# One loop over all decode units, one joining of the heads, and weights on 112 partitions

## The chip, the cores and the metric

The kernel runs on one core of a Trainium2 chip. The metric is the device time of one execution in microseconds. A time is the median of several runs; a profile is one further execution, recorded instruction by instruction and transfer by transfer.

## What is computed

One decode step for two sequences: an attention block over a cached key/value store and a two-layer ReLU network share the input `x` (2 x 448) and are mixed by a gate.

```python
g = sigmoid((x * gate_w).sum(-1, keepdims=True))
q = (x @ wq).reshape(2, 1, 16, 256).transpose(0, 2, 1, 3)
p = softmax(q @ k_cache^T * 256 ** -0.5)      # k_cache: 2 x 16 x 4096 x 256
a = (p @ v_cache) -> 2 x 1 x 4096 @ wo        # v_cache: 2 x 16 x 4096 x 256
b = relu(x @ w1) @ w2                         # w1: 448 x 1792, w2: 1792 x 448
out = g * a + (1 - g) * b
```

Everything is float32. The caches are 268 MB of the 290 MB that have to be read.

## The kernel before

A *unit* is one head of one sequence: 32 units. The host lays each out as 128 rows of 64 KB, the keys in the first half of a row, the values in the second (`kv[u]`). SBUF holds three such *slots* (`slot[0..2]`); unit u lies in slot u % 3.

**SyncE (SP)** issues all large loads. First wq into slot 2, then units 0 and 1 (L122 to L124), then in a loop of ten rounds with three units each the units 2 to 31 (`more`, L126). Before each refill it takes `free[s]`, which VectorE gives after the last use of the slot. Then `late` (L141): w1, the eight pieces `w1x`, and w2 into slot 2 once unit 29 is done there; wo in five pieces (`CUTS`) into slot 0 once unit 30 is done there. All of these go through one queue, in this order, over the core's 16 transfer engines. ScalarE issues only the small `xg` (x and gate_w).

448 input rows are laid out as three blocks of 128 and one of 64 (`KF` = 3 full blocks, `HP` = 64): the last block stands twice in `xg`, and the halves of wq and w1 that belong to it are spread over the upper and the lower 64 partitions, so that both weights fill 128 partitions (56 KB and 24.5 KB on each). `w1x` holds the last 448 columns of w1: those of the upper 64 partitions are laid on the lower 64 (`MOVE`), in eight transfers of eight partitions each.

**A unit** passes four engines. TensorE (`scores`, L243) waits for the slot (`land[s]`), for the unit's query and for `room` in the PSUM tile `ps`, and makes 4096 scores as 4 groups of 1024, each group repeated on 32 partitions. VectorE (`values`, L268) takes the maximum (L270); ScalarE (`softmax`, L261) takes the exponential (L263) and copies the next query into `query[s]` (`pick`, L257); VectorE multiplies the values with the probabilities and sums them, in eight instructions (L274), into `ov`. The first of them gives `room`, the last gives `free[s]`. TensorE, ScalarE and VectorE run this in ten rounds of three units; units 30 and 31 follow unrolled.

**Before the loop**: the gate by small matmuls (L196 to L208), the queries by wq in two halves (`NB` = 2, L217), each with transposes through `ident`. `xr` and `xu` are copies of x spread over columns, made by VectorE (L176, L178).

**The heads are joined twice** (`combine`, L294), for units 0 to 15 between the loop and the last two units, for units 16 to 31 at the end: two transposes of maxima and sums, the common maximum, exponentials, weights `wb` (with the gate in them), a matmul that spreads them, the weighting `os`, and matmuls with `sel` that sum the groups into `ot`.

**The end**: w1 (L336 to L345), ReLU, transposes, then 14 blocks of w2 and 24 blocks of wo are accumulated in the PSUM tile `acc`, the last eight blocks of wo directly in `z` (`project`, L372), while the second `combine` runs step by step between the wo blocks. `acc` is folded into `z`, copied and stored.

Every wait is written out: `pr.op` counts an engine's instructions in a semaphore of its own, and `take` waits on a semaphore and lowers it again.

Of the kernel before, what the change touches and what calls it, by code (L numbers as in the profile page):

```python
# [8 lines left out]
P, HP = 128, 64  # L9
G = 4  # L10
R = P // G
SLOTS = 3
NB = 2
ENGINES = ("tensor", "vector", "scalar", "gpsimd", "sync")


class Program:

    def __init__(self, nc):
        self.nc = nc
        self.code = {e: [] for e in ENGINES}
        self.count = dict.fromkeys(ENGINES, 0)

    def op(self, engine, fn, *after):
        self.count[engine] += 1  # L30
        self.code[engine].append(("op", fn, after))
        return engine, self.count[engine]

    def raw(self, engine, fn, *after):
        self.code[engine].append(("raw", fn, after))

    def loop(self, engine, n, fn):
        self.code[engine].append(("loop", n, fn))

    def emit(self, block, sems):  # L40
        def run(name):
            def body(e):
                seen = {}
                for kind, a, b in self.code[name]:
                    if kind == "loop":
                        with e.Fori(0, a) as i:
                            b(e, i)
                        continue
                    for who, n in b:
                        if seen.get(who, 0) < n:  # L50
                            e.wait_ge(sems[who], n)
                            seen[who] = n
                    if kind == "op":
                        a(e).then_inc(sems[name], 1)
                    else:
                        a(e)
            return body

        for name in ENGINES:
            getattr(block, name)(run(name))  # L60
# [7 lines left out]
def gated_mix_decode(nc, xg, kv, wq, w1, w1x, w2, wo, out):  # L68
    U, _, LEN = kv.shape
    KC, B = xg.shape[1], xg.shape[2] - 1  # L70
    KF = KC - 1
    D = KF * P + HP
# [5 lines left out]
    SG = S // G  # L78
    NF = w2.shape[1] // D
    DG = D // G  # L80
    FG = NF * P // G
    RB = R // B
    HB = H // NB
    UB = U // NB
    HH = HB // G
    CW = 512
    SCALE = float(DH) ** -0.5
    LOOPS = (U - 2) // SLOTS
    assert U == LOOPS * SLOTS + 2 and SLOTS == 3

# [3 lines left out]
    def bank(name, n=CW):  # L94
        return nc.alloc_psum_tensor(name, [P, n], F32).ap()

    NO = NB * HH * J
    CUTS = (0, NO - 18, NO - 8, NO - 4, NO - 1, NO)
    TAIL = 8
    names = [*ENGINES, "xg", "w1x", "w2", *(f"wo{k}" for k in CUTS[1:]), "query", "score", "top", "prob", "room",  # L100
             *(f"land{s}" for s in range(SLOTS)), *(f"free{s}" for s in range(SLOTS)), "out"]
    sem = {n: nc.alloc_semaphore(n) for n in names}
    land = [sem[f"land{s}"] for s in range(SLOTS)]
    free = [sem[f"free{s}"] for s in range(SLOTS)]
    pr = Program(nc)
    pe, dve, act, pool, sp = ENGINES


    sbuf("gap", P, -(-(-nc.sbuf_base // 32) * 32) % 1024 // 4)
    slot = [sbuf(f"slot{s}", P, LEN) for s in range(SLOTS)]  # L110
    ps = bank("ps", SG)
    pw = [bank(f"pw{k}") for k in range(4)]
    acc = bank("acc")[:, :D]


    def load(s, src, signal, lo=0, hi=None):
        hi = src.shape[1] if hi is None else hi
        return lambda e: e.dma_start(slot[s][:, lo:hi], src[:, lo:hi]).then_inc(signal, 16)  # L118

    xg_sb = sbuf("xg_sb", P, KC, B + 1)  # L120
    pr.raw(act, lambda e: e.dma_start(xg_sb, xg).then_inc(sem["xg"], 16))
    pr.raw(sp, load(2, wq, land[2]))  # L122
    for u in range(2):
        pr.raw(sp, load(u, kv[u], land[u]))  # L124

    def more(e, i):  # L126
        for k in range(SLOTS):
            s = (2 + k) % SLOTS
            take(e, free[s])
            src = kv[bass.ds(i * SLOTS + (2 + k), 1)].rearrange("o p n -> (o p) n")  # L130
            e.dma_start(slot[s], src).then_inc(land[s], 16)

    pr.loop(sp, LOOPS, more)

    W1, WX = w1.shape[1], w1x.shape[2]
    w1_sb, w1x_sb = slot[2][:, :W1 + WX], slot[2][:, W1:W1 + WX]
    w2_sb = slot[2][:, W1 + WX:W1 + WX + NF * D]

    def late(e):  # L141
        take(e, free[2])
        load(2, w1, land[2])(e)
        for k in range(8):
            o = k // 4 * 4 * 8 + k % 4
            e.dma_start(w1x_sb[o:o + 4 * 7 + 1:4], w1x[k]).then_inc(sem["w1x"], 16)
        e.dma_start(w2_sb, w2).then_inc(sem["w2"], 16)
        take(e, free[0])
        for lo, hi in zip(CUTS, CUTS[1:]):
            load(0, wo, sem[f"wo{hi}"], lo * D, hi * D)(e)  # L150
        take(e, free[1])

    pr.raw(sp, late)

    ident = sbuf("ident", P, P)

    have_ident = pr.op(pool, lambda e: e.memset(ident, 0.0))
    have_ident = pr.op(pool, lambda e: e.affine_select(
        out=ident, in_=ident, compare_op=ALU.not_equal, fill=1.0, base=0, pattern=[[-1, P]], channel_multiplier=1),
        have_ident)  # L160


    sel = sbuf("sel", P, R)
    t = pr.op(dve, lambda e: e.tensor_reduce(sel, ident.rearrange("p (g r) -> p r g", g=G), axis=AX.X, op=ALU.add),
              have_ident)
    fsum = sbuf("fsum", P, B)
    t = pr.op(dve, lambda e: e.tensor_reduce(fsum, sel.rearrange("p (b r) -> p b r", b=B), axis=AX.X, op=ALU.add), t)
    fold = sbuf("fold", P, B, RB)
    have_fold = pr.op(dve, lambda e: e.tensor_scalar(fold, fsum[:, :, None].to_broadcast([P, B, RB]), 1.0 / RB, None,
                                                     op0=ALU.mult), t)  # L170


    xr = sbuf("xr", P, KC, G, B, RB)
    pr.raw(dve, lambda e: e.wait_ge(sem["xg"], 16))
    for g in range(G):
        pr.op(dve, lambda e, g=g: e.tensor_copy(xr[:, :, g], xg_sb[:, :, :B, None].to_broadcast([P, KC, B, RB])))  # L176
    xu = sbuf("xu", P, KC, UB // B, B)
    have_x = pr.op(dve, lambda e: e.tensor_copy(xu, xg_sb[:, :, None, :B].to_broadcast([P, KC, UB // B, B])))  # L178

    def rows_of(c, i=0):  # L180
        return slice(0, P) if c < KF else slice(i * HP, (i + 1) * HP)

    def flat(a):
        return a.rearrange("p b r -> p (b r)")

    def mm(out, lhs, rhs, start, stop, *after):
        return pr.op(pe, lambda e: e.matmul(out, lhs, rhs, start=start, stop=stop), *after)  # L187

    def transpose(out, src, *after):
        return pr.op(pe, lambda e: e.transpose(out, src, ident), *after)  # L190

    def activate(out, src, fn, *after, **kw):
        return pr.op(act, lambda e: e.activation(out, src, fn, **kw), *after)  # L193


    pr.raw(pe, lambda e: e.wait_ge(sem["xg"], 16))  # L196
    for c in range(KC):
        r = rows_of(c)
        t = mm(pw[0][:, :1], xr[r, c].rearrange("p g b r -> p (g b r)"), xg_sb[r, c, B:], c == 0, c == KC - 1, have_x)
    gp = sbuf("gp", P, 1)  # L200
    gate_read = t = activate(gp, pw[0][:, :1], AF.Sigmoid, t)
    omg = sbuf("omg", P, 1)
    have_omg = pr.op(dve, lambda e: e.tensor_scalar(omg, gp, -1.0, 1.0, op0=ALU.mult, op1=ALU.add), t)
    for c in range(KC):
        r = rows_of(c)
        t = mm(pw[1][:UB, :1], xu[r, c].rearrange("p u b -> p (u b)"), xg_sb[r, c, B:], c == 0, c == KC - 1)
    gu = sbuf("gu", UB, 1)
    have_gu = activate(gu, pw[1][:UB, :1], AF.Sigmoid, t)  # L208


    qt = sbuf("qt", P, T, U)
    W = 2 * KF * DH
    WQ = wq.shape[1] // NB
    wide = sbuf("wide", P, CW)
    pr.raw(pe, lambda e: take(e, land[2], 16))
    busy = [(), ()]
    for i in range(NB):  # L217
        w = slot[2][:, i * WQ:(i + 1) * WQ]
        for c in range(KC):
            for g in range(G):  # L220
                r = rows_of(c, g // 2)
                at = g * W + c * CW if c < KF else G * W + g % 2 * CW
                lhs, rhs = flat(xr[r, c, g]), w[r, at:at + CW]
                last = mm(pw[2 + i][g * R:(g + 1) * R, :], lhs, rhs, c == 0, c == KC - 1)
        t = activate(wide, pw[2 + i], AF.Copy, last, *busy[1], scale=SCALE)
        pt = pw[i]
        for k in range(2 * T):
            t2 = transpose(pt[:, k * P:(k + 1) * P], wide[:, k * P:(k + 1) * P], t, gate_read, have_gu)
        busy[1] = (t2,)
        for s in range(2):  # L230
            dst = qt.rearrange("p t (i g s b) -> p i s t g b", i=NB, g=G, s=2)[:, i, s]
            src = pt[:, ::RB].rearrange("p (s t g b) -> p s t g b", s=2, t=T, g=G)[:, s]
            have_q = activate(dst, src, AF.Copy, t2)

    nm = sbuf("nm", P, U)
    ls = sbuf("ls", P, U)
    ov = sbuf("ov", P, U, J)
    prob = sbuf("prob", P, SG)  # L240
# [20 lines left out]
    def softmax(e, u, s, more=True):  # L261
# [3 lines left out]
        if more:  # L265
            pick(e, u + 1, (s + 1) % SLOTS)
# [200 lines left out]
```

## Time and profile before

| | |
|---|---|
| median of 3 runs | 675.29 us (675.29 to 675.54) |
| span of the profiled execution | 674.6 us |
| moved in it | 289.66 MB, 429 GB/s over the span |
| busy: VectorE, TensorE, ScalarE | 341.5, 224.6, 59.7 us |
| TensorE clock granted | 0.648 of full speed |

The span runs from the first to the last instruction of the profiled execution; the runs' times have about 0.7 us more around it. In the views below, PE is TensorE (PEld its weight loads), DVE is VectorE, ACT ScalarE, POOL GpSimd and SP SyncE; `L274` is line 274 of the kernel; `out<-in` are the program's names. A group's row gives the number of its instructions, busy microseconds and the mean of one in nanoseconds, then the idle time ahead of them and what ended it. A row of the timeline or of the chain begins with its start and its length in microseconds. A row of a stretch gives start and end, its length, busy time and instructions of PE, PEld, DVE, ACT and POOL, the granted clock, the share of time that the 16 transfer engines were busy, and GB/s. A row of a load gives its size and the microseconds from issue to landing.

### The profile page before, as it was taken

How to read it: one execution, taken by the hardware profiler on the slowest of the kernel's cores; microseconds unless marked ns; L12 is line 12 of the kernel's file. 1: busy time of each engine (PE TensorE's matmuls, PEld its weight loads, DVE VectorE, ACT ScalarE, POOL GpSimd, SP SyncE). 2: the span in 40 equal slices, each digit the busy share in tenths (PEclk: the TensorE clock that was granted, in tenths of full speed). 3: DMA queues.
4: the chain of work that ended last, by engine and by line, in shares of the span. 5: the costliest groups of instructions: out<-in, count | busy, mean ns of one | idle time of the engine just before them, and what ended most of it. 6: DMA issues, size and time to landing. Idle time of an engine off the chain costs nothing. (4 is left out here: it accounts for less than half of the span.)

```text
span 674.6 us, 4166 instructions
## 1 busy us (share of the span) xinstructions
PE 224.6 (33%) x1323; PEld 67.0 (10%) x1323; DVE 341.5 (51%) x571; ACT 59.7 (9%) x121; POOL 0.7 (0%) x6
## 2 busy tenths in 40 slices
PE   0643221333332123333322333333222333321277
PEld 0210000001001000100100010010001001000022
DVE  0006566544556664455566545455665544657652
ACT  0020001001000100100010010000001001000010
POOL 0000000000000000000000000000000000000000
PEclk9975567667655666765566676665567666556688
DMA  9999999999999999999999999999999999999997
GB/s 381 428 435 436 436 435 435 435 435 435 435 431 435 435 435 435 435 431 435 435 435 435 435 435 435 435 435 435 435 435 435 435 431 427 435 427 435 400 444 316
DMA packets 6180, 289.66 MB, mean 429 GB/s; under 512 B 992, under 2 KB 1120, under 8 KB 1440
## 3 DMA queue, kind: packets, MB, share of 16 engines
q1 hardware_dynamic: 6032, 289.60, 99.3%
q8 instruction: 3, 0.05, 0.0%
q10 hardware_dynamic: 144, 0.01, 0.0%
q14 instruction: 1, 0.01, 0.0%
HBM read 289.54 MB, written 0.06 MB: 429 GB/s over the span
## 5 line engine op out<-in xcount | busy, mean ns | idle before, releaser
L274 DVE SCALAR_TENSOR_TENSOR slot<-slot,prob 128x1024 f32<-128x1024 f32 x256 | 295.9, 1222 | 65.1 <-DVEq L65 65.1
L251 PE MATMUL ps<-slot,query 128*32 128x512 f32 x1024 | 190.8, 909 | 404.4 <-PEq L65 404.3
L270 DVE TENSOR_REDUCE nm<-ps 128x1024 f32 (+1 forms) x32 | 39.2, 1225 | 230.8 <-DVEq L65 230.8
L251 PEld LDWEIGHTS ps<-slot,query 128*32 128x32 f32 x1024 | 54.7, 158 | 539.1 <-issue 539.0
L263 ACT ACTIVATE prob<-ps,nm 128x1024 f32<-128x1024 f32 x32 | 35.6, 1113 | 385.0 <-ACTq L65 384.9
L263 ACT ACT_TABLE_LOAD x10 | 12.8, 1283 | 163.4 <-ACTq L65 163.4
L274 DVE DVE_READ_ACCUMULATOR slot<-slot,prob (+1 forms) x256 | 21.3, 83 | 0.0
L187 PE MATMUL pw<-slot,xr 128*32 128x512 f32 (+3 forms) x96 | 12.9, 671 | 1.3 <-DMA slot<-in_w1x 1.3
L176 DVE COPY xr<-xg_sb 128x128 f32<-128x128 f32 x4 | 0.6, 224 | 18.0 <-DMA xg_sb<-in_xg 18.0
L187 PE MATMUL pw<-xg_sb,xr 128*128 128x1 f32 (+1 forms) x8 | 1.9, 352 | 21.2 <-DVE xu L178 21.2
L187 PE MATMUL acc<-slot,ot 128*32 128x448 f32 x48 | 7.2, 661 | 2.3 <-DMA slot<-in_wo 2.2
L258 ACT ACTIVATE query<-qt 128x2 f32 (+1 forms) x32 | 6.2, 193 | 0.0
L263 ACT ACTIVATION_READ_ACCUMULATOR prob<-ps,nm (+1 forms) x32 | 6.2, 193 | 0.0
L187 PE MATMUL acc<-slot,hr 128*32 128x448 f32 x28 | 4.9, 810 | 2.0 <-DMA slot<-in_w 2.0
L190 PE MATMUL pw<-ident,nm 128*16 128x128 f32 x2 | 0.7, 328 | 12.6 <-DVEq L324 12.6
L187 PEld LDWEIGHTS pw<-xg_sb,xr 128*128 128x128 f32 (+1 forms) x8 | 1.8, 321 | 21.2 <-DMA xg_sb<-in_xg 21.2
L187 PEld LDWEIGHTS pw<-slot,xr 128*32 128x32 f32 (+1 forms) x96 | 2.8, 122 | 9.9 <-issue 7.7
L190 PE MATMUL pw<-ident,wide 128*128 128x128 f32 x11 | 1.9, 288 | 2.4 <-ACT wide L193 2.4
L310 DVE TENSOR_TENSOR os<-ov,pw 128x128 f32<-128x128 f32 x2 | 0.6, 287 | 4.0 <-PE pw L187 4.0
L318 DVE COPY ot<-pw 128x256 f32<-128x256 f32 x4 | 1.5, 420 | 2.0 <-PE pw L187 2.0
L391 DVE COPY wide<-acc 128x448 f32<-128x448 f32 x1 | 0.6, 624 | 3.1 <-PE pw L187 3.1
L187 PE MATMUL pw<-slot,ot 128*32 128x112 f32 x64 | 2.0, 261 | 0.2 <-DMA slot<-in_wo 0.2
(42 smaller groups left out, 20.9 us busy)
## 6 DMA issues: line engine op xcount, KB each, us to landing
slot<-in_wq SPq DMA_DIRECT2D x1, 7168.0 KB, 19.4
slot<-in_w SPq DMA_DIRECT2D x1, 3136.0 KB, 29.9
slot<-in_wo SPq DMA_DIRECT2D x1, 3136.0 KB, 21.2
slot<-in_w SPq DMA_DIRECT2D x1, 2912.0 KB, 28.2
slot<-in_wo SPq DMA_DIRECT2D x1, 2240.0 KB, 26.1
slot<-in_wo SPq DMA_DIRECT2D x1, 896.0 KB, 27.8
slot<-in_wo SPq DMA_DIRECT2D x1, 672.0 KB, 28.9
slot<-in_kv SPq DMA_DIRECT2D x32, 38.4
```

The costliest lines, as they stand in the source:

```text
L176: pr.op(dve, lambda e, g=g: e.tensor_copy(xr[:, :, g], xg_sb[:, :, :B, None].to_broadcast([P, KC, B, RB])))
L187: return pr.op(pe, lambda e: e.matmul(out, lhs, rhs, start=start, stop=stop), *after)
L190: return pr.op(pe, lambda e: e.transpose(out, src, ident), *after)
L251: m = e.matmul(ps[g * R:(g + 1) * R, c * CW:(c + 1) * CW], query[s][:, t:t + 1].to_broadcast([P, R]), slot[s][:, lo:lo + CW], start=(t == ...
L258: e.activation(query[s], qt[:, :, bass.ds(u, 1)].rearrange("p t o -> p (t o)"), AF.Copy).then_inc(sem["query"], 1)
L263: e.activation(prob, ps, AF.Exp, bias=nm[:, bass.ds(u, 1)], accum_out=ls[:, bass.ds(u, 1)]).then_inc(sem["prob"], 1)
L270: e.tensor_reduce(nm[:, bass.ds(u, 1)], ps, axis=AX.X, op=ALU.max, negate=True).then_inc(sem["top"], 1)
L274: m = e.scalar_tensor_tensor(v, v, 1.0, prob, op0=ALU.mult, op1=ALU.mult, accum_out=ov[:, bass.ds(u, 1), j])
L310: t = pr.op(dve, lambda e: e.tensor_tensor(os, ov[:, us], wp[:, :UB, None].to_broadcast([P, UB, J]), op=ALU.mult), t)
L318: t = pr.op(dve, lambda e, hh=hh: e.tensor_copy(ot[:, i, hh], po[:, hh * B * J:(hh + 1) * B * J].rearrange("p (b j o) -> p j b o", j=J, o= ...
L391: t = pr.op(dve, lambda e: e.tensor_copy(a_sb, acc), t)
```

## The change

The program is written anew engine by engine, without the counting class. What it does otherwise:

- `x`, wq and w1 are laid out as four blocks of 112 rows (448 = 4 x 112) on 112 partitions: wq is 64 KB and w1 28 KB on each. `w1x` is gone. kv, w2 and wo stay on 128 partitions.
- The gate's sums are made by GpSimd and one matmul with ones; GpSimd also makes `xr`, then `ident`, and `xo` (x times 1 - g), so that the ReLU network's part of the gate is in its input. The attention's part of the gate is applied when `lhs` is written.
- All 32 units run in one loop: eleven rounds on TensorE, the third unit of a round under a test; on VectorE and ScalarE one unit a round. VectorE computes the slot's address from the unit's number.
- There is one `query` tile and no `room`.
- The last unit's keys and values are two transfers with a semaphore each (`land[1]`, `late`); VectorE waits for the values before it multiplies.
- All 32 units are joined once: TensorE transposes maxima and sums after the last exponential, VectorE does the softmax part between the last unit's products (after the fourth and the seventh, under tests of the unit's number), and the rest follows after the loop. All 24 + 8 wo blocks come after it.
- wo comes in pieces of 14, 6, 4, 4, 3 and 1 blocks (before: 14, 10, 4, 3 and 1).

```diff
-P, HP = 128, 64
+P, KP = 128, 112
...
-        for k in range(8):
-            o = k // 4 * 4 * 8 + k % 4
-            e.dma_start(w1x_sb[o:o + 4 * 7 + 1:4], w1x[k]).then_inc(sem["w1x"], 16)
...
+    def sync(e):
+        bring(e, slab(2, 0, KC * NQ * G * CW, KP), wq, sem["wq"])
+        for u in range(2):
+            bring(e, slot[u], kv[u], land[u])
+        with e.Fori(0, U // SLOTS) as i:
+            for k in range(SLOTS):
+                take(e, sem["free"])
+                s = (k + 2) % SLOTS
+                src = kv[bass.ds(i * SLOTS + (k + 2), 1)].rearrange("o p n -> (o p) n")
+                if k < SLOTS - 1:
+                    bring(e, slot[s], src, land[s])
+                    continue
+                with e.If(i == U // SLOTS - 1):
+                    bring(e, slot[s][:, :T * S], src[:, :T * S], land[s])
+                    bring(e, slot[s][:, T * S:], src[:, T * S:], sem["late"])
+                with e.Else():
+                    bring(e, slot[s], src, land[s])
+        take(e, sem["free"])
+        bring(e, slab(2, 0, KC * F, KP), w1, sem["w1"])
+        bring(e, slab(2, W2, LEN), w2, sem["w2"])
+        take(e, sem["free"])
+        for lo, hi in zip(WO, WO[1:]):
+            bring(e, slab(0, (lo - NF) * D, (hi - NF) * D), wo[:, (lo - NF) * D:(hi - NF) * D], sem[f"wo{hi}"])
...
+    def gpsimd(e):
+        e.memset(ones, 1.0)
+        e.memset(qt[:, :, U:], 0.0)
+        e.wait_ge(sem["xg"], 16)
...
+        e.tensor_copy(xc4, xg_sb[:KP, :, :B, None].to_broadcast([KP, KC, B, RB]))
+        settle(e, sem["pool"], e.memset(ident, 0.0))
...
+        with e.Fori(0, -(-U // SLOTS)) as i:
+            for s in range(SLOTS - 1):
+                scores(s)
+            with e.If(i < U // SLOTS):
+                scores(SLOTS - 1)
+        take(e, sem["query"])
+        e.transpose(tp[:U, :P], nm, ident)
+        e.transpose(tp[:U, P:2 * P], ls, ident).then_inc(sem["tr"], 1)
+        take(e, sem["xo"])
+        take(e, sem["w1"], 16)
+        project(xo, 0, F)
+        take(e, sem["wb"])
...
+        with e.Fori(0, U) as u:
+            take(e, sem["score"], G)
+            e.tensor_reduce(nm[:, bass.ds(u, 1)], ps, axis=AX.X, op=ALU.max, negate=True).then_inc(sem["top"], 1)
+            take(e, sem["prob"])
+            with e.If(u == U - 1):
+                e.wait_ge(sem["late"], 16)
+            for j in range(J):
+                v = ring[:, bass.ds((u % SLOTS) * LEN + (T * S + j * SG), SG)]
+                m = e.scalar_tensor_tensor(v, v, 1.0, prob, op0=ALU.mult, op1=ALU.mult,
+                                           accum_out=ov[:, bass.ds(u, 1), j])
+                if j == 3:
+                    with e.If(u == U - 1):
+                        take(e, sem["tr"])
+                        e.tensor_reduce(nb, mt, axis=AX.X, op=ALU.min).then_inc(sem["nb"], 1)
+                if j == 6:
+                    with e.If(u == U - 1):
+                        take(e, sem["e4"])
...
+            m.then_inc(sem["free"], 1)
+        settle(e, sem["vec"], e.drain())
+        take(e, sem["wp"])
+        e.tensor_tensor(os, ov, wp[:, :, None].to_broadcast([P, U, J]), op=ALU.mult).then_inc(sem["os"], 1)
...
-    w1x = np.concatenate([w1[:HP, -MOVE:], w1[HP:, -MOVE:]], 1)
...
+        return a.reshape(KC, KP, -1).transpose(1, 0, 2)
...
+    wq = rows(wq.reshape(D, -1)).reshape(KP, -1)
...
+    w1 = rows(B_w1).reshape(KP, -1)
```

`bring` is a transfer with its semaphore, `settle` an instruction that its own engine waits for, `slab(s, lo, hi, rows)` a part of slot s.

## Prediction before the changed kernel was run

> **What bounds the kernel now.** I read the page first: its DMA lines, the chain that ended last and the costliest groups.
>
> ```profile
> span 674.6 us, 4166 instructions
> ...
> DMA  9999999999999999999999999999999999999997
> GB/s 381 428 435 436 436 435 435 435 435 435 435 431 435 435 435 435 435 431 435 435 435 435 435 435 435 435 435 435 435 435 435 435 431 427 435 427 435 400 444 316
> ...
> q8 instruction: 3, 0.05, 0.0%
> ...
> DMA slot<-in_wo 4%; SPq L118 0%; PE pw L187 0%; DVE res L397 0%
> ...
> L274 DVE SCALAR_TENSOR_TENSOR slot<-slot,prob 128x1024 f32<-128x1024 f32 x256 | 295.9, 1222 | 65.1 <-DVEq L65 65.1
> ...
> slot<-in_wq SPq DMA_DIRECT2D x1, 7168.0 KB, 19.4
> ...
> slot<-in_w SPq DMA_DIRECT2D x1, 2912.0 KB, 28.2
> ...
> slot<-in_kv SPq DMA_DIRECT2D x32, 38.4
> slot<-in_w1x SPq DMA_DIRECT2D x8, 28.0 KB
> ```
>
> The transfer engines are busy in every slice and the chain ends in the loading of wo; no compute engine is above 51%. Stretches of the span, with the DMA share and GB/s last, show where anything could be won:
>
> ```profile
> 0.00:20.20 20.20, 0.00 (x0) 0.00 (x0) 0.74 (x3) 1.28 (x1) 0.70 (x6) 1.00 1.00 416
> 20.20:39.50 19.30, 13.04 (x88) 5.02 (x88) 0.89 (x6) 2.25 (x9) 0.00 (x0) 0.96 1.00 435
> 39.50:620.50 581.00, 179.10 (x962) 51.71 (x962) 314.61 (x513) 52.00 (x101) 0.00 (x0) 0.62 1.00 433
> 620.50:639.80 19.30, 7.40 (x42) 2.27 (x42) 10.62 (x21) 1.30 (x3) 0.00 (x0) 0.59 0.96 415
> 639.80:655.80 16.00, 10.73 (x79) 3.10 (x83) 8.73 (x16) 2.65 (x6) 0.00 (x0) 0.82 1.02 437
> 655.80:671.60 15.80, 13.38 (x124) 4.20 (x116) 5.64 (x15) 0.26 (x1) 0.00 (x0) 0.79 0.92 387
> 671.60:674.60 3.00, 0.97 (x32) 0.71 (x32) 0.27 (x1) 0.00 (x0) 0.00 (x0) 1.00 0.08 21
> ```
>
> From 20 to 656 us the stream runs at its plateau of 435 GB/s. One unit (8192 KB, 8.39 MB) takes 8.39/0.435 = 19.3 us; wq (7168 KB, 7.34 MB) 16.9 us; w1 with w1x (2912 + 8 x 28 = 3136 KB, 3.21 MB) 7.4 us. The change moves the same bytes, so nothing in compute counts unless it makes this stream pause or slow down.
>
> **Units in one loop, VectorE unit by unit: nothing.** One unit in the steady part, in the timeline:
>
> ```profile
> 331.16 58.34 SPq L131 DMA_DIRECT2D slot<-in_kv  x4
> ...
> 331.29 5.41 PE L251 MATMUL ps<-slot,query 128*32 128x512 f32 x32 [12.86 <-PEq L65]
> ...
> 336.99 1.23 DVE L270 TENSOR_REDUCE nm<-ps 128x1024 f32 x1 [6.08 <-DVEq L65]
> 338.40 1.28 ACT L263 ACT_TABLE_LOAD   x1 [16.90 <-ACTq L65]
> ...
> 350.31 0.08 DVE L274 DVE_READ_ACCUMULATOR slot<-slot,prob  x1
> ...
> 350.67 5.88 PE L251 MATMUL ps<-slot,query 128*32 128x512 f32 x32 [13.97 <-PEq L65]
> ```
>
> VectorE works from 336.99 to 350.39, 13.4 of 19.3 us: 5.9 us a unit are free. The unit's slot is free 19.1 us after its keys came; the refill lies 38.4 us in the queue, of which 19.3 are its own transfer, so another 19.1 us could pass before the queue runs dry. Added per unit: three tests and a computed slot address on VectorE, a loop end on VectorE and ScalarE, and a table load in each unit instead of in one of three (1.28 us by its row). The tests have no row; bounds are 0 and, at one VectorE instruction (1.22 us) each, 3.7 us. With the table load that is 5.0, under 5.9: I take 0. Without that cover each microsecond over it would cost 32 us. The semaphore "room" goes, since the next scores wait for a query that is copied only after the exponential has read them; PE starts no later by it.
>
> **The start: nothing.** The same timeline, from xg's arrival:
>
> ```profile
> 20.34 0.63 DVE L176 COPY xr<-xg_sb 128x128 f32<-128x128 f32 x4 [18.04 <-DMA xg_sb<-in_xg]
> ...
> 23.46 5.78 PE L187 MATMUL pw<-slot,xr 128*32 128x512 f32 x32
> ...
> 36.19 24.03 SPq L131 DMA_DIRECT2D slot<-in_kv  x2
> 39.88 5.97 PE L251 MATMUL ps<-slot,query 128*32 128x512 f32 x32 [4.03 <-PEq L65]
> ```
>
> The four copies into xr, the copy into xu and two sets of gate matmuls go; seven GpSimd instructions stand between xg's arrival and the query products instead, and the transposes wait for ident, now made behind xg on the same engine. GpSimd's own rows lie at 0.1 to 0.3 us (0.70 for six in the first stretch); taking 0.1 and 1.22 as bounds, seven cost 0.7 to 8.5 us against the 3.1 us that now pass from 20.34 to 23.46: at most 5.4 later. Waiting behind it are SP's refill of slot 2, issued at 36.19, and the first scores. The queue still holds two units (20.2 + 38.6 = 58.8), 22 us of cover. If it were gone, the excess would be lost once.
>
> **The end: nothing from joining once, or from keys and values apart.** The timeline from unit 29's last product on:
>
> ```profile
> 619.67 5.48 SPq L146 DMA_DIRECT2D slot<-in_w1x  x8
> ...
> 641.15 0.08 DVE L274 DVE_READ_ACCUMULATOR slot<-slot,prob 128x1 f32 x1
> 641.33 2.23 SPq L118 DMA_DIRECT2D slot<-in_wo  x5
> ...
> 647.04 1.23 DVE L270 TENSOR_REDUCE nm<-ps 128x1 f32<-128x1024 f32 x1 [5.80 <-DVEq L65]
> ...
> 658.90 0.09 DVE L274 DVE_READ_ACCUMULATOR slot<-slot,prob 128x1 f32 x1
> ...
> 660.38 0.15 DVE L301 TENSOR_REDUCE nb<-pw 16x1 f32<-16x4 f32 x1 [1.39 <-PE pw L190]
> ...
> 662.53 1.72 PE L187 MATMUL acc<-slot,ot 128*32 128x448 f32 x8 [2.19 <-DMA slot<-in_wo]
> ...
> 666.10 4.19 PE L187 MATMUL acc<-slot,ot 128*32 128x448 f32 x32
> ...
> 666.54 0.76 DVE L318 COPY ot<-pw 128x256 f32<-128x256 f32 x2 [1.43 <-PE pw L187]
> ```
>
> The chain that ended last, in order of time, closes so:
>
> ```profile
> 642.65 28.93 DMA slot<-in_wo
> 671.59 0.04 issue
> 671.63 1.10 PE pw L187 x32
> ```
>
> With keys 9.6 us ahead, unit 31's scores run under unit 30's products (end 641.23), and its own 11.9 us on VectorE (647.04 to 658.99) start there: 653.2. Joining now takes from 660.38 to 667.3, 6.9 us with waits for PE; double width on all of it would be 13.8, and 667.0. Without the wo products that PE now slips in between, and with the softmax part moved into the value loop, I take 5 to 6, near 659. The first piece of wo lands at 662.5: 3.5 us of cover. Queued behind the wait for ot are 24 wo blocks (48 passes; 32 took 4.19 us by the same timeline, about 6.3 in all) and the closing products; late by the upper bound they would still be fed by pieces that land until 671.6, so the tail would grow by 2 us at most. VectorE's new waits for "late", "tr" and "e4" hold the rest of unit 31's products and only PE's joining behind them. On SP eight issues (5.48 us) go and two come (0.33 to 0.43 each), all while it waits for slots. Moving 224 KB of w1 to the lower 64 partitions is undone: 14 KB for each of eight engines, 0.5 us at 27.2 GB/s (435/16), either way; I take 0.
>
> **112 partitions: 12.1 us.** The bytes stay, but wq becomes 64 KB on each of 112 partitions instead of 56 KB on 128, w1 28 KB instead of 24.5. The trace has no 112-partition load; the w1x pieces are its only narrow ones, and at 640 to 656 us, where they pass, the rate is 437. Lower bound: equal bytes, equal time, 0 (not below: the stream already stands on its plateau). Next: time follows the bytes of one partition. A unit's 64 KB take 19.3 us, so wq takes 19.3, +2.4, and w1 8.4, +1.05: **+3.5**. [...]
>
> [...]
>
> **Sum:** span 674.6 + 0 + 0 + 0 + 12.1 = 686.7; the median of the runs shown (675.29) lies 0.7 above the span: **687.4 us**.
>
> **The rivals.** *Bytes of a partition alone* (+3.5): 678.8. For it: the unit's 19.3 us at 64 KB. Against it: it needs engines that never hold each other up. *112 partitions cost nothing* (0): 675.3. For it: w1x passes without a dent. Against it: those pieces are 224 KB beside the 128-partition w2. *Faster:* the stretches 620.5 to 639.8 and 655.8 to 671.6 move 415 and 387 GB/s; if w1x's eight issues and the uneven ends that they leave make this loss, dropping them gives back up to 19.3 x 20/435 + 15.8 x 48/435 = 2.6 us, 672.7; it decides only where 112 partitions cost under 1.3. Against it: the small last pieces of wo stay. *Code fetched again in each turn of the loops:* three 16 KB code packets now (0.05 MB); one a unit on one engine is 0.6 us at 27.2 GB/s, 32 x 0.6 = 19.3, 694.6. Or VectorE's 5.9 us are passed by one, 707. Against both: three-unit bodies fetch almost nothing today. [...]
>
> **Chances.** Held-up engines (own range 682 to 692) 0.52, a partition's bytes 0.26, no cost 0.12, faster 0.04, fetches or VectorE 0.06. A measurement of this kernel can tell 0.2% (1.35 us): slower 0.52 + 0.26 + 0.06 + 0.02 of the no-cost case = 0.86; same 0.10; faster 0.04. The range takes in the second case and most of the first: 676 to 692.
>
> **What would show it.** Right: the rate falls well below 416 GB/s in the first 20 to 30 us and again where w1 loads, the first unit's scores start some 8 us after 39.88, refills still reach landing after about 38 us, and the chain still ends in wo. Half right: wq 2.4 us later and no more. Wrong: a plateau unchanged at both places. Units more than 19.3 us apart with VectorE never waiting, or many more code packets, would be the last rival.

## Result: 22 us slower, nearly all of it where 112 partitions are loaded

| | median | runs | ratio to before, 95% interval |
|---|---|---|---|
| before | 675.54 us | 5 (675.29 to 675.86) | |
| changed | 697.41 us | 5 (695.85 to 699.88) | 1.0327 (1.0307 to 1.0346) |

The profiled execution of the changed kernel took 695.85 us, with a span of 694.5 us (674.6 before). A time lies 1.3 us above its span here and in every run that lists both; the 0.7 given with the kernel before compares a median with the span of another execution. The page of the changed kernel:

```profile
span 694.5 us, 4431 instructions
...
DMA  9999999999999999999999999999999999999997
GB/s 242 242 449 427 449 427 423 442 434 449 427 423 434 442 449 423 427 430 442 434 442 427 423 445 430 449 427 423 442 434 449 427 423 434 442 449 406 341 357 303
...
q8 instruction: 3, 0.05, 0.0%
```

The transfer engines count as busy in every slice, as before, but in the first two slices they move 242 GB/s, where the kernel before moved 381 and 428, and in slices 38 and 39 they move 341 and 357, where it moved 400 and 444. So a busy share near one says that engines have work, not that it flows: below, the share is 1.03 at 259 GB/s. Between, the plateau is the old one. The number of code packets is unchanged.

The two dents are the two loads on 112 partitions. The loads of the changed kernel, with size and us from issue to landing (the row `in_w` is w1 and w2 together):

```profile
ring<-in_w SPq DMA_DIRECT2D x2, 3136.0 KB, 36.5
...
ring<-in_kv SPq DMA_DIRECT2D x31, 37.7
...
ring<-in_wq SPq DMA_DIRECT2D x1, 33.4
```

Its stretches, with start and end, length, busy time of PE, PEld, DVE, ACT and POOL, granted clock, share and GB/s:

```profile
1.80:33.40 31.60, 0.00 (x0) 0.00 (x0) 0.00 (x0) 0.00 (x0) 0.00 (x0) 1.00 1.03 259
...
34.20:53.50 19.30, 10.53 (x78) 3.65 (x80) 0.74 (x3) 3.24 (x8) 1.67 (x7) 0.93 1.00 435
53.50:635.00 581.50, 173.09 (x968) 43.65 (x972) 314.39 (x510) 77.43 (x120) 0.00 (x0) 0.64 1.00 434
...
650.60:666.00 15.40, 0.58 (x2) 0.14 (x2) 12.02 (x21) 2.83 (x5) 0.00 (x0) 0.54 1.00 250
```

wq lands 33.4 us after its issue, against 19.4 before: 14.0 us. While w1's rows move (650.6 to 666.0), the rate is 250 GB/s. In the 600 us between, unit follows unit at the old rate.

The timeline of the changed kernel, from xg's arrival, through its first unit, and at the end:

```profile
34.38 0.20 POOL L145 TENSOR_TENSOR pg<-xg_sb 112x8 f32<-112x8 f32 x1 [33.39 <-DMA xg_sb<-in_xg]
...
37.72 5.11 PE L169 MATMUL ph<-ring,xr 112*32 112x512 f32 x32 [1.69 <-PEq L19]
...
53.46 5.77 PE L184 MATMUL ps<-ring,query 128*32 128x512 f32 x32 [4.01 <-PEq L19]
59.58 1.23 DVE L277 TENSOR_REDUCE nm<-ps 128x1024 f32 x1 [22.16 <-DVEq L19]
61.00 1.28 ACT L256 ACT_TABLE_LOAD   x1 [11.12 <-ACTq L19]
...
73.30 0.08 DVE L283 DVE_READ_ACCUMULATOR ring<-ring,prob  x1
73.33 6.08 PE L184 MATMUL ps<-ring,query 128*32 128x512 f32 x32 [14.10 <-PEq L19]
...
676.36 1.23 DVE L302 TENSOR_TENSOR lhs<-po,gate 128x1024 f32<-128x1024 f32 x1 [0.76 <-DVEq L19]
681.75 4.72 PE L221 MATMUL acc<-ring,lhs 128*32 128x448 f32 x40 [1.04 <-DMA ring<-in_wo]
...
690.93 0.98 PE L232 MATMUL z<-ring,lhs 128*32 128x112 f32 x32
692.48 0.27 DVE L308 COPY res<-z 128x112 f32<-128x112 f32 x1 [3.81 <-DVEq L19]
```

The first unit's scores start at 53.46 instead of 39.88, 13.6 us late, and the queue never regains it. The last products start at 690.93 instead of 671.63, 19.3 us late: 5.7 us more were lost on the way, most of them at w1, whose rows take 1.9 us each by the median where they take 1.06 in the padded kernel below. The remaining 0.6 of the span's 19.9 us lie behind them.

### The profile page after: what moved, and what is told of

It reads as the page before. It is cut to its first block, busy times and chain, and to the rows that moved or that the text cites. A ratio compares the mean times of both kernels' runs of the same rounds, so it can differ in the third digit from the quotient of the medians.

```text
span 694.5 us, 4431 instructions
## 1 busy us (share of the span) xinstructions
PE 214.4 (31%) x1294; PEld 56.9 (8%) x1294; DVE 339.1 (49%) x556; ACT 87.3 (13%) x140; POOL 2.1 (0%) x13
## 5 line engine op out<-in xcount | busy, mean ns | idle before, releaser
L283 DVE SCALAR_TENSOR_TENSOR ring<-ring,prob 128x1024 f32 x256 | 296.0, 1221 | 105.4 <-DVEq L19 105.4
L184 PE MATMUL ps<-ring,query 128*32 128x512 f32 x1024 | 183.3, 881 | 416.9 <-PEq L19 416.9
L277 DVE TENSOR_REDUCE nm<-ps 128x1024 f32 x32 | 39.2, 1225 | 189.2 <-DVEq L19 189.2
L184 PEld LDWEIGHTS ps<-ring,query 128*32 128x32 f32 x1024 | 46.2, 155 | 553.3 <-issue 553.3
L283 DVE DVE_READ_ACCUMULATOR ring<-ring,prob x256 | 21.1, 82 | 0.0
L221 PE MATMUL acc<-ring,lhs 128*32 128x448 f32 x76 | 10.3, 628 | 1.5 <-DMA ring<-in_wo 1.5
L169 PE MATMUL ph<-ring,xr 112*32 112x512 f32 x64 | 8.8, 696 | 1.7 <-PEq L19 1.7
L169 PE MATMUL ph<-ring,xo 112*32 112x512 f32 x32 | 6.2, 952 | 8.8 <-PEq L19 8.8
L256 ACT ACTIVATION_READ_ACCUMULATOR prob<-ps,nm x32 | 6.2, 193 | 0.0
L221 PEld LDWEIGHTS acc<-ring,lhs 128*32 128x32 f32 x76 | 2.8, 123 | 8.3 <-issue 4.6
## 6 DMA issues: line engine op xcount, KB each, us to landing
ring<-in_kv SPq DMA_DIRECT2D x31, 37.7
```

The lines of the kernel that those rows point to most:

```text
L169: m = e.matmul(ph[g * R:(g + 1) * R], x[:KP, c], slab(2, at, at + CW, KP), start=c == 0, stop=c == KC - 1)
L184: m = e.matmul(ps[g * R:(g + 1) * R, c * CW:(c + 1) * CW], query[:, t:t + 1].to_broadcast([P, R]), slot[s][:, at:at + CW], start=t == 0, s ...
L221: m = e.matmul(acc[g * R:(g + 1) * R], lhs[:, k], w, start=k < G, stop=k >= N - DIRECT - G)
L256: e.activation(prob, ps, AF.Exp, bias=nm[:, bass.ds(u, 1)], accum_out=ls[:, bass.ds(u, 1)]).then_inc(sem["prob"], 1)
L277: e.tensor_reduce(nm[:, bass.ds(u, 1)], ps, axis=AX.X, op=ALU.max, negate=True).then_inc(sem["top"], 1)
L283: m = e.scalar_tensor_tensor(v, v, 1.0, prob, op0=ALU.mult, op1=ALU.mult, accum_out=ov[:, bass.ds(u, 1), j])
```

## Experiments

**One part undone: 128 partitions in the new kernel.** Everything of the rewrite stays; x, wq and w1 are laid out in three full blocks and one half block.

```diff
-P, KP = 128, 112
+P, HP = 128, 64
...
-                    at = base + c * step + g * CW
-                    m = e.matmul(ph[g * R:(g + 1) * R], x[:KP, c], slab(2, at, at + CW, KP), start=c == 0,
+                    at = base + c * step + g * CW if c < KF else last + g % 2 * CW
+                    r = slice(0, P) if c < KF else slice(g // 2 * HP, (g // 2 + 1) * HP)
+                    m = e.matmul(ph[g * R:(g + 1) * R], x[r, c], ring[r, 2 * LEN + at:2 * LEN + at + CW], start=c == 0,
```

> The rewritten kernel with everything kept but x, wq and w1 laid on 128 partitions again (three full blocks and one half block, its halves on the upper and lower 64; w1 padded by 64 columns on each partition instead of the eight w1x pieces). Theory A, the 112 partitions alone cost the 22 us: about 675.5 us, within 1.5 of the kernel before, and the first unit's scores start again near 40 us. Rival R, the one loop, the single joining and the gate on GpSimd cost a part: it stays above 677, by as much as they cost.

Measured: 676.63 us (10 runs, 676.24 to 676.94), ratio 1.0009 (1.0000 to 1.0019). Its first unit's scores start where they did in the kernel before:

```profile
39.91 5.82 PE L187 MATMUL ps<-ring,query 128*32 128x512 f32 x32 [3.83 <-PEq L20]
```

Of the 21.9 us, 20.8 go with the 112 partitions. Theory A holds within its 1.5 us; rival R's 677 is not reached, but about a microsecond stays. (w1's padding is 128 columns on each partition, not 64: 3200 KB instead of 3136, worth 0.15 us at 435 GB/s.)

**112 rows loaded as 128.** The four blocks of 112 stay, products and all; the loads bring 16 rows of zeros along.

```diff
-        bring(e, slab(2, 0, KC * NQ * G * CW, KP), wq, sem["wq"])
+        bring(e, slab(2, 0, KC * NQ * G * CW), wq, sem["wq"])
...
-        bring(e, slab(2, 0, KC * F, KP), w1, sem["w1"])
+        bring(e, slab(2, 0, KC * F), w1, sem["w1"])
...
+    wq, w1 = (np.concatenate([a, np.zeros((P - KP, a.shape[1]), a.dtype)]) for a in (wq, w1))
```

> The rewritten kernel with its four blocks of 112 rows, but 16 rows of zeros are loaded too, so that wq and w1 are 128-partition loads of 64 KB and 28 KB a partition (8.39 and 3.67 MB). Theory A as 'engines get in each other's way on 112 rows': that is gone and only the bytes of a partition are left, 3.5 us over the 128-partition layout, about 679 us. Rival B, 112 rows themselves are slow whatever the transfer's shape (the layout, the products on 112 rows): it stays near 697.

Measured: 680.19 us (4 runs, 679.94 to 680.98), ratio 1.0064 (1.0047 to 1.0081). More bytes, 17 us less, and wq lands 22.2 us after its issue instead of 33.4:

```profile
ring<-in_wq SPq DMA_DIRECT2D x1, 22.2
```

The loss is in the shape of the load, not in 112 rows of products. What is left over the 128-partition layout, 680.19 - 676.63 = 3.6 us, is as expected (3.5). But the padded loads also move 1.44 MB more (291.17 against 289.73 MB), 3.3 us at 435 GB/s, so this run doesn't tell "a partition's bytes" from plain bytes.

**Only wq padded.** The first change and the last line of that diff, for wq alone.

> As the padded kernel, but only wq is padded; w1 stays a load of 112 rows of 28 KB. Theory A: wq's loss goes (it landed 14.0 us later than before; the padding keeps 2.4 of these), w1's stays: 697.4 - 14.0 + 2.4 = 686 us. Rival: the loss at w1 was only the engines' disorder left by wq, and goes with it: 680 us.

Measured: 685.32 us (4 runs, 684.38 to 686.05), ratio 1.0140 (1.0122 to 1.0157). w1 on 112 partitions loses by itself: 685.32 - 680.19 = 5.1 us against w1 padded, 6.2 with the 1.05 that w1's padding costs (an estimate: 0.46 MB of zeros at 435 GB/s). So w1's loss is not the disorder that wq leaves.

**Loads alone.** Rows of 64 KB, each line below waited for before the next (the waits are left out here, and a last load of 128 rows like the first).

```python
for name, n in (("a128", 128), ("a112", 112), ("a96", 96), ("a64", 64), ("a120", 120)):
    load(ring[:n], src[name])
load(ring[16:128], src["u112"])
load(ring[:112], src["p112"][:, :ROW])                                # source rows 68 KB apart
for j in range(7): load(ring[j:j + 7 * 15 + 1:7], src["c112"][...])   # 16 rows, seven apart
for j in range(7): load(ring[j * 16:(j + 1) * 16], src["d112"][...])  # 16 adjacent rows
load(ring[0:29:4], src["n8"])                                         # 8 rows, four apart
load(ring[0:33:4], src["n9"])
```

> No attention at all: twelve loads of rows of 64 KB, one after the other, each waited for, and the output is zeros; it leaves out the whole computation. Shapes: 128, 112, 96, 64, 120 rows; 112 rows on partitions 16 to 127; 112 rows whose source rows lie 68 KB apart; 112 rows as seven loads of 16 rows seven partitions apart; as seven loads of 16 adjacent rows; 8 rows and 9 rows four partitions apart; 128 rows again. Theory P (engines that write the same group of partitions at once slow each other): 128 rows 21 us with the landing, 112 rows 32, the same with the source rows 68 KB apart and as seven loads seven partitions apart; seven loads of 16 adjacent rows much slower, up to 67 us, since four engines meet in each group; 9 rows twice as long as 8. Rival H (the order in which 112 rows are read from HBM): 112 rows with the source 68 KB apart near 19 us, 16 adjacent rows near 19, 9 rows as long as 8.

The stretches from the first to the last row of each load, up to the sixteen adjacent rows, in the order of the code (the columns are start and end, length, DVE, POOL, clock, share, GB/s):

```profile
1.70:22.70 21.00, 0.00 (x0) 0.00 (x0) 1.00 0.95 399
24.00:56.10 32.10, 0.00 (x0) 0.00 (x0) 1.00 0.95 229
57.50:88.00 30.50, 0.00 (x0) 0.00 (x0) 1.00 0.98 206
89.80:110.70 20.90, 0.00 (x0) 0.00 (x0) 1.00 0.97 201
112.40:153.70 41.30, 0.00 (x0) 0.00 (x0) 1.00 0.92 190
155.10:186.70 31.60, 0.00 (x0) 0.00 (x0) 1.00 0.96 232
188.40:219.70 31.30, 0.00 (x0) 0.00 (x0) 1.00 0.93 228
221.50:252.60 31.10, 0.00 (x0) 0.00 (x0) 1.00 0.96 236
254.10:320.00 65.90, 0.00 (x0) 0.00 (x0) 1.00 0.98 111
```

128 rows go at 399 GB/s with their start; 112, 96 and 64 rows at 229, 206 and 201, though they are fewer bytes, and 120 rows take 41 us. Rows 68 KB apart in the source change nothing (31.3), other partitions neither (31.6): theory H falls. Seven loads of 16 rows, seven partitions apart, take the same 31.1, as they would if 112 rows are dealt to sixteen engines in sevens, one after the other. Seven loads of 16 adjacent rows take 65.9, more than twice that, and near theory P's 67. 9 rows take 5.4 us where 8 take 3.4: longer, as theory P says, but not twice as long. The last load of 128 rows takes 21.0 again. So it matters which partitions are written at once: 31.1 or 65.9 us for 112 rows.

**Who is held up.** The seven steps of a 112-row load one by one, and small loads. The groups of the two theories are an assumption of the author: no trace here tells which partitions form one, and what is read below are the lengths of the transfers.

```diff
+        for j in range(7):
+            load(ring[j:j + 7 * 15 + 1:7], src["c112"][j * 16:(j + 1) * 16])
+            done()
+        for n in (8, 9, 12, 16):
+            load(ring[0:4 * n - 3:4], src[f"n{n}"])
+            done()
```

> Loads alone again, output zeros, the whole computation left out. 128 rows; 112 rows; the seven steps of the 112-row load one by one, each waited for (16 rows seven partitions apart, 64 KB a row); single loads of 8, 9, 12 and 16 rows four partitions apart; then four loads of 8, 12 and 16 such rows queued together. Theory P1 (only the engines that share a group are slowed, the others run on): each of the seven steps takes twice a row's time plus the landing, some 6.5 us, because a pair meets in each, but most of its sixteen transfers keep 2.4 to 3 us; in the load of 12 rows four transfers stay short. Rival P2 (a shared group holds up all engines): all sixteen transfers of a step take near 5 us, and in the load of 12 rows all twelve.

The stretches of the seven steps, then of 8, 9 and 12 rows (columns as above):

```profile
56.90:62.30 5.40, 0.00 (x0) 0.00 (x0) 1.00 0.85 194
64.10:69.30 5.20, 0.00 (x0) 0.00 (x0) 1.00 0.81 202
71.40:76.70 5.30, 0.00 (x0) 0.00 (x0) 1.00 0.78 198
78.70:83.80 5.10, 0.00 (x0) 0.00 (x0) 1.00 0.62 206
85.90:90.70 4.80, 0.00 (x0) 0.00 (x0) 1.00 0.65 218
92.90:98.10 5.20, 0.00 (x0) 0.00 (x0) 1.00 0.83 202
100.30:105.60 5.30, 0.00 (x0) 0.00 (x0) 1.00 0.82 198
107.70:111.30 3.60, 0.00 (x0) 0.00 (x0) 1.00 0.45 146
113.10:118.50 5.40, 0.00 (x0) 0.00 (x0) 1.00 0.35 109
120.50:126.00 5.50, 0.00 (x0) 0.00 (x0) 1.00 0.66 143
```

Steps four and five have a share of 0.62 and 0.65, the others 0.78 to 0.85: as long, but with fewer engines busy in them. The same in single transfers, one a row, sorted, in ns:

```
step 1:  4121 4168 4249 4268 4466 4471 4491 4553 4568 4672 4678 4682 4688 4944 5113 5148
step 4:  2415 2472 2547 2773 2981 3000 3019 3019 3056 3075 3132 3171 3318 3358 4539 4568
step 5:  2434 2472 2705 2715 2732 2764 2887 2999 3040 3056 3159 3207 3339 3433 4422 4636
8 rows:  2988 3104 3235 3264 3320 3320 3339 3358
9 rows:  2849 2868 3000 3047 3113 3142 3160 3929 4629
12 rows: 4434 4549 4681 4694 4706 4754 4771 4814 4839 5184 5187 5393
```

In steps four and five two transfers are long and fourteen are not (P1); in the other five all sixteen are long (P2). 9 rows make two long, 12 rows all twelve. So neither theory holds alone: in two steps and with 9 rows the slowness stays with two transfers, in the other five steps and with 12 rows it takes all of them. Four loads queued together give the same: with 8 rows each they take 10.6 us together, with 12 or 16 rows each 21.1 and 21.3.

The changed kernel's own load of wq has this pattern. Taken in sixteens by their start, the fourth and the fifth sixteen of its 112 rows have two rows at 4.4 to 4.8 us and fourteen at 3.2 to 3.8; the second, third, sixth and seventh have all sixteen at 4.2 to 4.9. So the order of the steps and the hold-up are those of the kernel too. What sets the two kinds of steps apart, no run here shows.

**What the rewrite itself costs.** 676.63 is 1.3 above the 675.36 of the kernel before, run beside it. The end of the 128-partition kernel:

```profile
669.01 0.62 DVE L309 COPY wide<-acc 128x448 f32<-128x448 f32 x1 [11.42 <-DVEq L20]
...
671.69 0.40 PE L232 MATMUL z<-wide,fold 128*32 128x112 f32 x8 [0.71 <-PEq L20]
...
671.88 0.97 PE L235 MATMUL z<-ring,lhs 128*32 128x112 f32 x32
673.43 0.28 DVE L311 COPY res<-z 128x112 f32<-128x112 f32 x1 [3.80 <-DVEq L20]
```

The copy of the accumulated tile ends at 669.63, but the fold, which needs nothing else, starts at 671.69, where the kernel before had it at 671.04: it is written behind the wait for the next piece of wo. And the last copy starts at 673.43, where it was 672.75.

```diff
             if k in WO:
                 e.wait_ge(sem[f"wo{WO[WO.index(k) + 1]}"], 16)
-            if k == N - 4:
-                take(e, sem["a"])
...
+            if k == N - 4:
+                e.wait_ge(sem["a"], 1)
...
-        take(e, sem["z"])
+        e.wait_ge(sem["z"], 1)
```

(The fold's block now stands ahead of the wait for wo; the wait for `acc` is changed like that for `z`.)

> The rewritten kernel on 128 partitions once more, beside the next one: 1.3 us above the kernel before.

> The rewritten kernel on 128 partitions with two edits at the end: the fold of the accumulated tile goes ahead of the wait for wo's three-block piece, and the three last waits of TensorE and VectorE no longer lower their semaphores. Theory T (what is left of the rewrite's cost is in the last 4 us, behind the last landing): 0.5 to 0.8 us under the 128-partition kernel, 675.9 us. Rival: the remainder lies ahead of the last landing, and nothing changes, 676.6.

Measured side by side: the 128-partition kernel 676.96 us (12 runs), ratio 1.0016 (1.0008 to 1.0025); with the edits 675.80 us (11 runs, 675.50 to 676.34), ratio 0.9999 (0.9991 to 1.0008). The end with the edits:

```profile
670.58 0.38 PE L230 MATMUL z<-wide,fold 128*32 128x112 f32 x8
...
671.38 0.97 PE L235 MATMUL z<-ring,lhs 128*32 128x112 f32 x32 [0.43 <-DMA ring<-in_wo]
672.43 0.28 DVE L311 COPY res<-z 128x112 f32<-128x112 f32 x1 [3.12 <-PE z L235]
```

1.2 us come back, more than theory T's 0.5 to 0.8, and nothing measurable is left of the rewrite's own cost. From the end of the last products (a modelled end) to the copy pass 0.08 us with the edits and 0.58 without, and the last products start 0.50 us earlier, 0.3 of it because the last piece of wo landed earlier in this execution. So both edits seem to have a share; they were not run apart, and how much each gives is open. This is the best version found; it equals the kernel before and doesn't beat it.

## Why the prediction was right in kind and wrong in size

**The bound** was read rightly: the stream of loads sets the time, and between the two loads the plateau never changed. The signs that the prediction named came: the rate fell at both places, the first scores were late (13.6 us where some 8 were put), and refills still landed after 37.7 us. Only that the chain still ends in wo can't be read: in the changed kernel that view breaks off at the last copy.

**Loops, start and joining at no cost** held. VectorE's unit takes 13.8 us (59.58 to 73.38) instead of the 13.4 of a unit with a table load, out of 19.3, and now each unit has one. From xg's arrival to the first query product pass 3.3 us, where 3.1 passed. `lhs` is written by 677.6, the first piece of wo is used at 681.75. On 128 partitions, where the stream is not late, `lhs` is written by 657.6 (659 was put) and wo is first used at 662.55. That kernel with the tail mended takes as long as the kernel before (0.9999), so these terms come to nothing in sum; they were not run one by one.

**The end** was put at nothing because the order of the last products was taken as the old one. The new code has the fold behind the wait for the next piece; I read over it. With the waits that lower their semaphores it cost 1.2 us by the runs, and it lay on the path.

**112 partitions: 12.1 us** is the step that failed, in its size and in the way that the size was reached. That the rows of a load on 112 partitions get slower is what the loads alone show: 4.6 us by the median, where 2.4 with 128 rows. But the size was the middle between 0 and 24.3, the price if wq and w1 took twice as long (16.9 + 7.4); the 24.3 and its half were the author's estimates, and no run shows either. Measured: wq +14.0 where 8.4 were put, w1 +6.2 where 3.7 were put, 20.2 together; with the tail's 1.2 that is 21.4 of 21.9. The middle assumed that half of the rows run on undisturbed. In five of seven steps none does: all sixteen take 3.5 to 5.1 us instead of the 2.4 of a row in a 128-row load. The 24.3, every row at half rate, was much nearer to these 20.2, and the range ended short of the sum with it (675.3 + 24.3 = 699.6).

**The rivals.** "A partition's bytes" alone (3.5) is refuted by the 21.9. The padded kernel's 3.6 agrees with its price, but can't be told there from the price of the zeros that it loads. "112 partitions cost nothing" leaned on w1x passing without a dent; those loads are of eight rows four partitions apart, and alone such a load has no long row (3.0 to 3.4 us, 8 rows in the last table). "Code fetched again" falls: three packets before and after. VectorE's 5.9 us are not used up. Of "faster" nothing shows in the ratio of 0.9999.

## What to carry to other kernels

A load that fills fewer than all 128 partitions can be slower than a larger one that fills them: 112 rows of 64 KB took 32.1 us where 128 took 21.0. A busy share near one doesn't show it (0.95 both times); the GB/s do (229 and 399). When a stream of loads sets the time, pad such a tensor to 128 rows or lay its remainder on both halves (680.19 and 676.63 us here instead of 697.41), and price an odd shape by a small load of its own before building on it. When bounds are far apart, don't take the middle: ask what one held-up transfer holds up in turn (with 9 rows two were long, with 12 rows all twelve).

## What had not been expected of the hardware

That in five of the seven steps all sixteen transfers are slow, where in the other two only two are (all sixteen at 4.1 us or more in step one, fourteen of sixteen under 3.4 in step four). Why stays open. And that the odder count can be the slower one: 120 rows took 41.3 us, 112 rows 32.1, 96 rows 30.5. The rows of the 120-row load took 5.1 us by the median, and 120 x 5.1 / 41.3 = 15 of them were under way at a time; for 112 rows it is 112 x 4.6 / 32.1 = 16.
